# Feed-forward rows kept in DRAM by chunk of tokens instead of by feature group, with the order of all streams written anew

## The chip, the cores and the metric

The kernel runs on one core of a Trainium2 chip. The metric is device time in microseconds for one execution, as the median of several runs; lower is better. The core has a matrix engine (TensorE, shown as PE; its weight loads as PEld), a vector engine (VectorE, DVE), an activation engine (ScalarE, ACT), a general engine (GpSimd, POOL) and a queue processor (SyncE, SP). DMA transfers are issued here from SP, ACT and POOL and run on sixteen DMA engines.

## The reference

What is computed is the forward pass and the gradients of one block over 2048 tokens of 512 channels. The input is normalized; one branch is a long convolution whose kernel comes from a diagonal state space model of 128 states for each channel, the other a feed-forward network of 1792 features; the two are multiplied and added to the input. Cut to what matters:

```python
def _B_ref(x, w1, w2):
    h = jnp.einsum("bsd,df->bsf", x, w1)
    h = _silu(h)
    out = jnp.einsum("bsf,fd->bsd", h, w2)
    return out
...
x = A_u
xn = _layernorm(x, axis=-1)
s = _A_ref(xn, A_A_re, A_A_im, A_B_re, A_B_im, A_C_re, A_C_im, A_log_dt, A_Dskip)
g = _silu(_B_ref(xn, B_w1, B_w2))
return x + s * g
```

`_A_ref` builds the convolution's kernel K from the parameters, and convolves it with its input by Fourier transforms. The outputs are the block's result and the gradients with respect to the input, the seven parameter arrays of the state space model, the skip vector `Dskip`, and the two weights `w1` and `w2`, for a given `grad_out`.

## The kernel before

The 2048 tokens are worked on in eight chunks of 256, the 1792 features in 14 groups of 128, the 512 channels in four blocks of 128. The program is a set of some forty-five streams, each a Python generator that issues a small step of work at every call. `play` (L120) walks through a string of letters and advances the stream of each letter by one step. So the string `PLAN` is the order in which every engine's queue is filled. It has seven sections, one for each phase. Engines run in their own queue's order and wait for each other through semaphores. Two more tables go with it: `SLOTS` says which of a tag's buffers each new tile takes, and `WAYS` says for each copy out of PSUM that goes through `Evac` (L107) whether ACT (A, issued at L116) or DVE (D, issued at L117) makes it.

The pre-activations h of the feed-forward network are needed three times, and are kept in a DRAM tile `k.Hd` in between:

- Written in the forward pass. `gen_ffn_fwd` (stream F) computes, for each chunk c, h transposed: features on the partitions and 256 tokens along the row, in tiles `hT` of eight groups and then six (L768 the products, `Evac` the copies, L776 the SiLU). After each tile, L778 stores it to `k.Hd` from POOL's queue (`k.st` is POOL's `dma_start`). That is 16 stores.
- Read by chunk in the gradient of the activations. `gen_da_loads` (stream a) loads tiles `dhT` of the same shape from SP's queue at L1141: 16 loads, with three buffers for the tiles of eight groups and two for those of six. Stream s turns them into the slope of SiLU on ACT (L1151), stream A multiplies them on DVE with the products of L1173 (L1176) and stores the result to `k.DHd` from SP (L1180), and stream x takes them to the gradient of the input (L1197).
- Read by feature group in the gradient of `w2`. `gen_dw2_loads` (stream h) loads, for each of the 14 groups, all 2048 tokens as one tile `h_in` at L1216, from SP's queue, into three buffers. Stream t turns each with TensorE in two halves of eight blocks (L138) and applies SiLU on ACT (L1227); stream w multiplies them with the output's gradient (L1236) and stores `out_11`.

Before the change `k.Hd` has the shape [14 groups, 128 partitions, 2048 tokens]. A store or load by chunk touches, for each partition and each group, a run of 256 tokens in DRAM, which is 512 bytes; a load by group touches one run of 2048 tokens, 4096 bytes, for each partition.

Other streams that the prediction names: V copies the products of the state space gradient out of PSUM (L1025), T multiplies them on DVE (L1042, L1046), S sums them on TensorE (L1062), and Z makes the parameter gradients from the sums (DVE L1086 to L1113, ACT L1121, POOL stores at L1124). Stream Y loads and turns tables for V. Streams g and v make the gradient of `w1` (loads with transposition of `k.DHd` at L1251, products at L1265). Streams i, k and m are the backward pass of the normalization at the very end; k runs on DVE (L1306, L1307, L1309) and ACT (L1313). Streams R, C and B make the convolution's kernel rows, the forward convolution and its gradient, J the turned chunks of the input, W the turned weights and d the turned output gradients. The kernel rows (stream R, L651 to L659) are made eight channel groups at a time, before and after.

Each stream's steps are the same before and after the change; only the places of the steps in the string are not.

Of the kernel before, what the change touches and what calls it, by code (L numbers as in the profile page):

```python
# [18 lines left out]
P = 128  # L19
# [5 lines left out]


PLAN = """
222315555166p567155737777617777p63677J360710734777p07J6760F3p67677J64FF7687J7F667F86676261F873776F03778FFFF47FF66667FF76
347674678F73F586F47688758/XXJPFJFFFXXXFXFXPXFQPFPFXFFPFFPFFFFPPFFFFF9FQJUUXFQQXJPXXQRQQXQQQFRFQPRRFRXFXFRXXPRFFPRRFFFPQF
UQRXXFFQFXFQFQPQQFUQFQFQRFFXFQXPXFPFXQRPXFRXRPRRRRRXPQRPFFFRPFRRRRRXFRFRXCQXXXQFXQQXQRQFQQRFQXXFRRUXFPRRQCRPFCPPFCFCCFCC  # L30
PCFQFJFQCQCCFQQFCQPFQCRRCCQQRCCFPXCXFQPCPJFXRFCFXRCFCPFCXFXFFFRCFRFQFRCFRFFRXFCXPCRRQQXFXRFCQCFRQFQQQRCRCRRQCQRCRRRCFQPC
XCXRRFCRRJPPXPXXRQJFXRPXQCQFQXFXFXQPQCRRQFQPQCPCRXFCCRFFQFCCCFCPCCFFRFFUFFCQCFFFCRCRCFCQRCFCCCRJCCRCQCXPXFXPCQCXRPCRCQXC
FXFCRQQPCRQPJCFRQCRCRFXCQPQCCXFFRFRXRQRXRFFXQCXRCPFFCRRFCFCRRCRFFFXXCQQCFCCFQFQQXFRXRRFRCCQCFUFXCQCQRCCQCRRRCRJCCRQRRCRJ
CRCCCRUCFCRCCRCRRFCRRFCC/CFCFCGGCGFGCCCGFFFCCFGCCCGGCGFCCFFCFGFCCCCGCFGGFWCCGFGCCCGHFCFCGHFCCFCGGFHCFCCGGCFCGCGCGCCCFCWG
CHWHWHWHCWCCCWWCDDGWCHCLCWMCWWWWDDWWDWDDWDWWWWLMWCDWDDWDLGDMDLMLWWM/DDEDDDDaaasdooEdWDdoDdDABAADooAABADsBDADAAaDAABAlABB
BBDDAABABAsDDAAaoBAABBBADODABBABOEBBABABDBBoDDBxsBDBBxBoBxBAAdBBBOoBAsAlDBOABxBdOEDBDoOlBxBaDxOoOBxOxODDBBDxxDBlABBsxBoB
ABBxoBAADBOAAOaBaoDBBBBBoDDBaAABBDAoDAdDBBAADBAdBABBAEAABABsBBAAODOABoOABBDBABEADODoDOxoDBAlDsOBoADDOAxAdBDDBOAoAdBADABB
BoxBAoOADsDxBABOOBBADBDOlaBoAAxOBDBDooxBBxBBaBAOxDxBABDoBDOsODBDADxBEBOBAAOdBOBoBABxxOAoAaBdABAoBBExBOAsBBBDDOBAaOBAxBAB
BBxxBOBAaBsBAaABxABABABBBBABxBAAAAABBBddBxsBABBBABBBAxBABsBAABB/NNAYNYNYANxxNAAVVsaYVVAdVVAVVVAdYVTAAYYAAVVVVVxAATAATsxV
VAAAxATVNxAAATNNAxTTTNNVAVVVTSSxVTAYAVxTTxVYVYxYTYSTTVVYTxVASVT/TVVVhYSVVVhTVVtttVtTVVVTSTYwVTttthVVVVYTYSwTtwVtVTVTTTVS  # L40
VwTVVTwYTZVStVtgZSTVTVtwNZYNwNgYTVYNVTwTTTvhSvtYvYthVtTVVTYZvtTSVwYvVVVVVZTSvVVYVSVZNvvTVZVZtTtTgYVTgVVwtVVTVStTVwTVwVTZ
vTwSVVZTVNVYTTVTVTwvZNVZTZZvSYVhZNYvTtYYvZNTSVVtvhtTtTYShYwTVVYvVtSVvVYVTVTtYZwTVVZwhTTTVTVVtSVYTtVwVVVtTSTwVtVVSVVSVwVV
YvTYVtTwTTtttZgTVwZTVZTZTTYYtvZVVgSVSZTTVZVZwVYZgvSZZYYhvvTSVtTZVhgVvvTwVTZVTVVwTVTZSTtgTTZTSvZgZTvtvStSwhtZwvZttwZZZtvZ
tZZvZZvvZZgZtv/ivwtkhkvvwkwitkivwvtvkkwmvtkmkvvktwgvvwvvitmkhmkikvvmkkmvgmtiwktkvkkvmgkwkvtvtwmmkivmmkvkkwkvvitmkmkmkkvv
vmkmmwmkkwvmmvwvmvvvmvm
""".replace("\n", "").split("/")
# [15 lines left out]

WAYS = """J=DDAADDAD;
F=ADAAAAAAADDAAADAAADAAAAAAAAAAADAAAAAAAAAAAAAADDAAADAAADADADDAAAAAADDAAAA;
X=AAAAAAAAAAAAAAAAAAAAAAAAAAAAAAAA;
U=AD;
R=AAAAAAAAAAAAAAADAADAAAAADAAAAAAA;
C=ADDADAAAAAAAAAAAAAAADDAAAAAAAADDAAAAADADAAADDADAADADDDADAAAAAAAA;  # L70
W=DDDDDDDDDDDDDD;
D=AAAADDAAAAAAAAADAAAAAAAAAAAAAAAAAADAAAAA;
d=DDDAADAA;
B=AAAAAAAAAAADAADAAAAAAAAADADAAAAAAAAAAAAADAAADAAAAAAADAAA;
x=AADDDAADAAAA;
V=ADDDAAADDDAAAAAADDAAAAADDAAAAAAAAAAAAAAAAAAAAAAAAAAAAAAAAAAAAAAA;
Y=AAAAADAA;
w=AAAAAAAADDAAAA;
v=DDDAAADDAAAAADDAAAAAAAAAAAAA"""
# [674 lines left out]
def gen_ffn_fwd(k):  # L754
    nc, fp = k.nc, k.fp
    D, FT, DK, T = k.D, k.FT, k.DK, k.T
    for c in range(T // 2):
        cs = slice(256 * c, 256 * c + 256)
        XTv = k.XT.pop(c)[:].rearrange("p (t k) n -> p t k n", k=DK)
        aT = fp.tile([P, FT, 256], BF16, name="aT", tag="aT", bufs=1)  # L760
        for f in range(FT // 2):
            if f in (0, 4):
                hT = fp.tile([P, 8, 256], BF16, name="hT", tag="hT", bufs=2)
            ps = k.pf.tile([P, 2, 256], F32, name="ps_h", tag="pf")
            for j in range(2):
# [4 lines left out]
            yield  # L770
            i = 2 * (f % 4)
            k.ev(hT[:, i:i + 2, :], ps[:])
            yield
            if f in (3, 6):
                f0, n = (0, 8) if f == 3 else (8, 6)
                nc.scalar.activation(out=aT[:, f0:f0 + n], in_=hT[:, 0:n], func=ACT.Silu)  # L776
                yield
                k.st(k.Hd[f0:f0 + n, :, cs].rearrange("f p n -> p f n"), hT[:, 0:n])  # L778
                yield
        late = c >= NS  # L780
        ob = k.do[:, 2 * c:2 * c + 2, :] if late else fp.tile([P, 2, D], BF16, name="ob", tag="ob", bufs=2)
        for t in range(2):
            ps = k.pf.tile([P, D], F32, name="ps_o", tag="pf")
            for ft in range(FT):
                nc.tensor.matmul(out=ps[:], lhsT=aT[:, ft, t * P:t * P + P], rhs=k.W2[:, ft, :],  # L785
                                 start=(ft == 0), stop=(ft == FT - 1))
            yield
            k.ev(ob[:, t], ps[:])
            yield
        if not late:  # L790
            k.st(k.Od[:, 2 * c:2 * c + 2, :], ob[:])
            yield
# [419 lines left out]
def gen_dw2_loads(k, fw):  # L1212

    for ft in range(k.FT):
        h = fw.tile([P, k.T, P], BF16, name="h_in", tag="h_in", bufs=3)
        k.nc.sync.dma_start(h[:].rearrange("p t n -> p (t n)"), k.Hd[ft])  # L1216
# [118 lines left out]
def kernel(ctx, tc, A_u, A_A_re, A_A_im, A_B_re, A_B_im, A_C_re, A_C_im, A_log_dt, A_Dskip, B_x, B_w1, B_w2, grad_out,  # L1335
           out_0, out_1, out_2, out_3, out_4, out_5, out_6, out_7, out_8, out_9, out_10, out_11):
    nc = tc.nc
    k = KCtx()
# [142 lines left out]
```

## Time and profile before

| what | value |
|---|---|
| runs of the kernel before | 576.57, 572.45, 576.95 us; median 576.57 |
| the profiled execution's own time | 576.9 us |
| its span, first to last instruction | 575.1 us |
| mean granted TensorE clock | 0.981 |
| DVE busy | 523.5 us (91%) |
| ACT busy | 442.6 us (77%) |
| POOL busy | 79.0 us (14%) |
| all DMA packets | 156643, 144.49 MB |

The profiled execution is 0.3 us above the median of the runs, and 1.8 us of it lie outside the span. A busy share is a mean over phases that have different limits; the prediction therefore reads the span in stretches. Idle time is given with what ended it ("releaser"). Some rows carry a line number of a helper: L116 and L117 are the ACT and DVE copies of `Evac` for all streams, L138 is the turning helper.

### The profile page before, as it was taken

What the parts mean: (1) busy time and instruction counts of PE and PEld (TensorE: products, weight loads), DVE (VectorE), ACT (ScalarE), POOL (GpSimd) and SP (SyncE); (2) the same over time, 40 slices, a digit from 0 to 9 for tenths busy, and PEclk for the clock granted to TensorE, in tenths of its full rate; (3) what the DMA queues carried; (4) which work ended last, traced back from release to release, by engine and by line L of the source; (5) the groups of instructions that cost most, each with busy time, mean ns of one, the idle gap of its engine ahead of it and who ended that gap; (6) DMA issues with size and microseconds to landing.
All of it is one profiled execution on the core that took longest, in us unless ns stands there. A gap on an engine that the chain in (4) does not pass through costs nothing.

```text
span 575.1 us, 14488 instructions
## 1 busy us (share of the span) xinstructions
PE 528.4 (92%) x5982; PEld 396.0 (69%) x6008; DVE 523.5 (91%) x821; ACT 442.6 (77%) x541; POOL 79.0 (14%) x164
## 2 busy tenths in 40 slices
PE   0788998999999999999999999999999999899895
PEld 0545777587777675877687866776678687767573
DVE  8999998999899969999999899869999999894984
ACT  6989998999988569998888876773667677642473
POOL 5341101011101021000000000000000300333031
PEclk9889998999999999999999999999999999999798
DMA  9988797798997999898789799898999989999653
GB/s 240 310 309 227 226 256 261 264 258 266 331 239 247 334 276 364 253 283 286 232 241 315 220 293 294 216 221 229 251 226 260 241 205 222 222 210 264 169 177 111
DMA packets 156643, 144.49 MB, mean 251 GB/s; under 512 B 83488, under 2 KB 132896, under 8 KB 153504
## 3 DMA queue, kind: packets, MB, share of 16 engines
q1 hardware_dynamic: 146816, 120.74, 76.0%
q0 software_dynamic: 6640, 19.67, 10.0%
q10 hardware_dynamic: 3120, 3.15, 1.7%
q8 instruction: 47, 0.77, 0.5%
q14 instruction: 20, 0.16, 0.1%
HBM read 62.78 MB, written 59.25 MB: 212 GB/s over the span
## 4 chain that ended last, share of the span: by engine, by line
PE 57%; DVE 15%; ACT 7%; issue 7%; DMA 7%; SPq 4%; POOL 2%; ACTq 0%; DVEq 0%; POOLq 0%
PE ps_da L1173 8%; PE ps_dx L1197 7%; PE ps_w L1236 7%; PE ps_w L1265 6%; PE ps_o L785 3%; PE ps_h L768 3%; PE ps_i L451 3%; PE pt_t L138 3%; PE ps_s L406 3%; DMA sp_in<-Ud 3%; PE ps_i L464 3%; PE ps_v L1025 2%; PE psS L1062 2%; PE ps_k L657 2%; PE ps_s L434 2%
## 5 line engine op out<-in xcount | busy, mean ns | idle before, releaser
L116 ACT CAST dA<-ps_s 128x1024 bf16<-128x1024 f32 x90 | 89.1, 1029 | 9.6 <-PE ps_s L434 4.1
L768 PE MATMUL ps_h<-XT,W 128*128 128x256 bf16 x448 | 59.4, 284 | 6.0 <-DVE XT L117 4.9
L1265 PE MATMUL ps_w<-dh_tok,xn 128*128 128x256 bf16 x448 | 55.2, 280 | 3.2 <-ACT o L116 3.2
L1173 PE MATMUL ps_da<-doT,W 128*128 128x256 bf16 x448 | 56.1, 273 | 0.4 <-DVE dhT L1176 0.4
L768 PEld LDWEIGHTS <-W 128*128 128x128 bf16 x448 | 44.1, 102 | 14.5 <-issue 7.1
L785 PE MATMUL ps_o<-W,aT 128*128 128x512 bf16 x212 | 50.8, 387 | 1.7 <-issue 0.5
L116 ACT CAST Vb<-ps_v 128x672 bf16<-128x672 f32 x54 | 38.5, 732 | 17.6 <-PE ps_v L1025 13.7
L1265 PEld LDWEIGHTS <-xn 128*128 128x128 bf16 x448 | 44.1, 100 | 10.1 <-issue 3.6
L1197 PE MATMUL ps_dx<-W,dhT 128*128 128x512 bf16 x224 | 51.0, 379 | 0.0
L1236 PE MATMUL ps_w<-YD,a_tok 128*128 128x512 bf16 x210 | 49.1, 379 | 0.7
L116 ACT CAST dB<-ps_i 128x1024 bf16<-128x1024 f32 x41 | 40.7, 1027 | 9.1 <-PE ps_i L451 9.1
L1173 PEld LDWEIGHTS <-W 128*128 128x128 bf16 x448 | 41.3, 98 | 8.3 <-issue 2.6
L1176 DVE TENSOR_TENSOR dhT<-ps_da,dhT 128x512 bf16<-128x512 f32 x56 | 37.7, 685 | 6.2 <-PE ps_da L1173 5.7
L785 PEld LDWEIGHTS <-aT 128*128 128x128 bf16 x224 | 21.6, 100 | 26.7 <-issue 3.1
L1197 PEld LDWEIGHTS <-dhT 128*128 128x128 bf16 x224 | 21.2, 98 | 24.1 <-issue 1.2
L1236 PEld LDWEIGHTS <-a_tok 128*128 128x128 bf16 x224 | 21.6, 98 | 23.2
L1227 ACT ACTIVATE a_tok<-pt_t 128x1024 bf16<-128x1024 bf16 x28 | 28.7, 1036 | 7.3 <-PE pt_t L138 7.3
L406 PEld LDWEIGHTS <-TF 128*128 128x128 bf16 x384 | 24.9, 100 | 12.1 <-ACT TF L288 4.4
L477 DVE TENSOR_TENSOR cm<-sp_in,dA 128x2048 bf16<-128x2048 bf16 x24 | 29.3, 1220 | 2.6 <-DMA sp_in<-Ud 1.7
L116 ACT CAST o<-ps_w 128x256 bf16<-128x256 f32 (+1 forms) x33 | 14.9, 451 | 20.0 <-PE ps_w L1265 10.7
L479 DVE TENSOR_TENSOR sp_in<-sp_in,dA 128x2048 bf16<-128x2048 bf16 x24 | 29.3, 1223 | 0.6
L584 ACT ACTIVATE sn<-V 128x1920 bf16<-128x1920 int16 x16 | 29.0, 1816 | 1.1 <-DVE V L580 1.0
(241 smaller groups left out, 1234.1 us busy)
## 6 DMA issues: line engine op xcount, KB each, us to landing
Yd<-YD SPq DMA_DIRECT2D x8, 1024.0 KB, 5.7
sp_in<-Ud SPq DMA_DIRECT2D x8, 1024.0 KB, 7.8
h_in<-Hd SPq DMA_DIRECT2D x14, 512.0 KB, 5.1
Ed<-ds SPq DMA_DIRECT2D x8, 672.0 KB, 6.3
Eb<-Ed SPq DMA_DIRECT2D x8, 672.0 KB, 5.1
Hd<-hT POOLq DMA_DIRECT2D x8, 512.0 KB, 7.7
Ud<-dA SPq DMA_DIRECT2D x8, 512.0 KB, 8.5
KXd<-dA SPq DMA_DIRECT2D x4, 1024.0 KB, 4.7
```

The costliest lines, as they stand in the source:

```text
L116: return self.nc.scalar.copy(out=out, in_=in_)
L406: nc.tensor.matmul(out=ps[:, j], lhsT=k.TF[:, 8 * h + j, c, :], rhs=U(8 * h + j), start=True, stop=True)
L477: TT(out=t2[:], in0=b[:, :, gs], in1=a[:, 1:2, gs].to_broadcast([P, 2, n, P]), op=ALU.mult)
L479: TT(out=b[:, :, gs], in0=b[:, :, gs], in1=a[:, 0:1, gs].to_broadcast([P, 2, n, P]), op=ALU.mult)
L584: nc.scalar.activation(out=sn[:, 0:n], in_=low, func=ACT.Sin, scale=-2 * PI_LO / 2.0 ** PB)
L768: nc.tensor.matmul(out=ps[:, j], lhsT=k.W1[:, dk, ft * P:ft * P + P], rhs=XTv[:, :, dk, :], start=(dk == 0), stop=(dk == DK - 1))
L785: nc.tensor.matmul(out=ps[:], lhsT=aT[:, ft, t * P:t * P + P], rhs=k.W2[:, ft, :], start=(ft == 0), stop=(ft == FT - 1))
L1173: nc.tensor.matmul(out=ps[:, j], lhsT=k.W2[:, ft, dk * P:dk * P + P], rhs=dTv[:, :, dk, :], start=(dk == 0), stop=(dk == DK - 1))
L1176: nc.vector.tensor_tensor(out=dh[:, i0:i0 + 2, :], in0=ps[:], in1=dh[:, i0:i0 + 2, :], op=ALU.mult)
L1197: nc.tensor.matmul(out=ps[:], lhsT=dhs[ft // 8][:, ft % 8, t * P:t * P + P], rhs=k.W1[:, :, ft * P:ft * P + P], start=(ft == 0), stop=(ft ...
L1236: nc.tensor.matmul(out=ps[:], lhsT=at[:, t, :], rhs=k.do[:, t, :], start=(t == 0), stop=(t == k.T - 1))
L1265: nc.tensor.matmul(out=ps[:], lhsT=k.xn[:, t, dk * P:dk * P + P], rhs=dh[:, t].rearrange("p j n -> p (j n)"), start=(t == 0), stop=(t == k ...
```

## The change

`k.Hd` gets the shape [8 chunks, 128 partitions, 14 groups, 256 tokens]. The store of a tile `hT` and the load of a tile `dhT` are then one run for each partition in DRAM: 4096 bytes for eight groups, 3072 for six. The load of one feature group, `h_in`, becomes eight runs of 512 bytes for each partition, one from each chunk. The bytes are the same everywhere, as are the queues: POOL for the stores, SP for both loads. No other instruction is added or taken away.

```diff
@@ gen_ffn_fwd @@
-                k.st(k.Hd[f0:f0 + n, :, cs].rearrange("f p n -> p f n"), hT[:, 0:n])
+                k.st(k.Hd[c][:, f0:f0 + n, :], hT[:, 0:n])
@@ gen_da_loads @@
-            k.nc.sync.dma_start(dh[:, 0:n], k.Hd[f0:f0 + n, :, 256 * c:256 * c + 256].rearrange("f p n -> p f n"))
+            k.nc.sync.dma_start(dh[:, 0:n], k.Hd[c][:, f0:f0 + n, :])
@@ gen_dw2_loads @@
-        k.nc.sync.dma_start(h[:].rearrange("p t n -> p (t n)"), k.Hd[ft])
+        k.nc.sync.dma_start(h[:].rearrange("p (c u) n -> p c (u n)", u=2), k.Hd[:, :, ft, :].rearrange("c p n -> p c n"))
@@ kernel @@
-    k.Hd = dr.tile([k.FT, P, L], BF16, name="Hd")
+    k.Hd = dr.tile([8, P, k.FT, 256], BF16, name="Hd")
```

With it the whole of `PLAN`, `SLOTS` and `WAYS` is written anew. The letters of each stream are the same in number over all sections, but some steps cross a boundary: section 4 (the fifth) holds 35 steps of V and 18 of T instead of 30 and 17, and section 5 has 101 of V instead of 106. The start of section 5, where the loads `h_in` begin, as an example:

```diff
-TVVVhYSVVVhTVVtttVtTVVVTSTYwVTttthVVVVYTYSwTtwVtVTVTTTVS
+hTVVTYVVSThYVtTtttSVYTTtVVSTYhwtVSTTTwVVVTtYVSwVVtTVVwhV
```

In `WAYS`, D stands 94 times before and 105 times after, of 454 copies. By stream, the copies that DVE makes: J 5 to 6, F 15 to 18, R 3 to 5, C 17 to 16, d 4 to 3, B 7 to 11, V 10 to 12, Y 1 to 2, w 2 to 4, v 7 to 5; the others keep their numbers.

More of the change, by code (lines that the diff above doesn't have):

```diff
@@ L32 @@
[L32 to L41, printed above, removed]
@@ new lines @@
+F75FF738F7FFFJ76F7F6778FJ34/XFXFFFXXXXXXPPPFPF9PFFPFFFPQFFFFXPFFXQQFUQFQQFFFQQUFPFFXRQXQXXPFXFFQXXRFQRPXFPRRXRUFFFFRPXFU
+QRXQRFFRXQFPFRFFQXFFJFQFQXQQFXXPFQQFFXPQRPRRPRXRRJFRRRFPFXQPRFPRRRRRRFFFXFXQRFFQCPXQXXXQQQRXFQFQRQFPRFRRXFCXCPPCRFURCCQC
+QQCCFCQFCFFQPCQQCPFCCQPRRQRCPJCCCQQJXFXFRCPCXFQFFCCCXFXFRXFFCFCFXFXRFRRFRCFRXFQFRFQRCQQCFQQRPCQRFFRCQRXFCRPCCQRQRCFRRCRX
+RPPCXRQRPCXFRXJRUPCJCRXQFXFXXPXQFCQXCPQQFXFQFPFRRCRQFCCQCFFCQQCCCPQFFFFRFFCRCFFCFCRRFCRCRJCCPCCCRCPCXFXFPXRCQXRCFXXQCRQC
+PQCQQPPQJCFXFCPRCQRCCRFQRCRCCFRXRFCRFXRQFQFXFXRCFXCCPRFCFRRCFFURFXRQXCCQQFCFQCCFXFRRJXQCRRFQCCFXQFQRQCCCCCCRRCRRRQCRRCCR
@@ L58 @@
+010110101101011010;dft.t4=010010101010;gate.g=10237456;gate.S=01;da.dhT8=01201201;da.dhT6=01010101;da.doT=10101010;go.go
+_s=01010101;go.go_r=010101;dftb.w8b=1010;go.go_g=01010101;go.go_x=01201201;da.pd_s=101010101010;sb.YT=2012012012012012;s
 b.Eb=01010101;sb.Gb=01010101;sb.Vb=0101010101010101;sb.Tp=0101010101010101;sb.Sa=1010;fw.h_in=01201201201201;fw.a_tok=10
-101010101010;fw.o11=01201201201201;fw.dh_tok=0120120;sb.g_acc=0101;fw.o10=0101010;lw.pd_l=012301;lw.Gt=01230123;lw.m=010
+101010101010;fw.o11=01201201021021;sb.g_acc=0101;fw.dh_tok=0120120;fw.o10=0101010;lw.pd_l=012301;lw.Gt=01230123;lw.m=010
@@ L60 @@
 101;lw.o1=12031203
 """.replace("\n", "").split(";") if x)
[L65 to L66 removed]
+WAYS = """J=DDADDDAD;
+F=DAAAAAAAADDDADAAAAAAAAAAAAAAAAAADAAAAAAAAAAAADDAAAADAADDADADAAAADDDDDAAA;
 X=AAAAAAAAAAAAAAAAAAAAAAAAAAAAAAAA;
 U=AD;
[L69 to L70 removed]
+R=AAAAAAAAAAAAAADDAAAAAAAADAADAADA;
+C=ADDADAAAAAAAAAAAAAAADDAAAAAAAADDAAAAADADAAADADAAADADDDADAAAAAAAA;
@@ L71 @@
 W=DDDDDDDDDDDDDD;
 D=AAAADDAAAAAAAAADAAAAAAAAAAAAAAAAAADAAAAA;
[L73 to L79, printed above, removed]
+d=DDAADAAA;
+B=AAAAAAAAAAADDADAAADAAAAADAAAAAADAAAADADAAAAADAAAAAAAADAD;
+x=AAADDAAADADA;
+V=ADADDDDAAAAAAAADAAAADAADAAAAAADAAADAAAAAAAAAAAAAAAAAADAAAAADAAAA;
+Y=AADDAAAA;
+w=DDAADAAAADAAAA;
+v=ADADAAAAAAAADDAAAAAAAAAAAADA"""
```

35 lines of the change are left out of this document (19 added, 16 removed).

## The prediction

> **What bounds the kernel now.** I read the page's busy times first, then the busy time of each engine in stretches, because a share of the whole span hides which engine is full where.
>
> ```profile
> span 575.1 us, 14488 instructions
> PE 528.4 (92%) x5982; PEld 396.0 (69%) x6008; DVE 523.5 (91%) x821; ACT 442.6 (77%) x541; POOL 79.0 (14%) x164
> ```
>
> PE and DVE are busy for nearly the same time. The table by stretches has a column for the length, then the busy time of PE, PEld, DVE, ACT and POOL with instruction counts, the granted clock, the DMA share and GB/s.
>
> ```profile
> 0.00:43.00 43.00, 22.94 (x154) 15.40 (x156) 40.07 (x103) 35.98 (x54) 18.96 (x68) 0.92 0.92 286
> 43.00:225.00 182.00, 171.12 (x2130) 129.24 (x2139) 170.26 (x217) 163.85 (x182) 22.23 (x28) 0.99 0.88 271
> 225.00:300.00 75.00, 73.75 (x977) 55.74 (x975) 73.36 (x100) 68.90 (x72) 2.18 (x4) 1.00 0.82 261
> 300.00:365.00 65.00, 65.00 (x778) 46.47 (x777) 60.36 (x81) 49.60 (x54) 4.30 (x8) 1.00 0.90 283
> 365.00:410.00 45.00, 43.76 (x451) 32.07 (x450) 37.70 (x53) 24.69 (x26) 0.00 (x0) 1.00 0.92 211
> 410.00:490.00 80.00, 78.67 (x856) 61.69 (x863) 79.07 (x122) 59.56 (x91) 9.02 (x17) 1.00 1.04 238
> 490.00:530.00 40.00, 37.81 (x383) 29.33 (x386) 28.25 (x63) 17.46 (x30) 14.30 (x26) 1.00 0.99 234
> 530.00:575.20 45.20, 35.36 (x265) 26.06 (x265) 34.42 (x88) 22.56 (x37) 7.96 (x14) 0.88 0.54 154
> ```
>
> The start belongs to DVE (40.07 of 43). From 43 to 225 PE, DVE and ACT are all at nine tenths or more. From 225 to 490 PE is idle for only 75.00+65.00+45.00+80.00 less 73.75+65.00+43.76+78.67, which is 3.8 us, and DVE is as full as PE in 225 to 300 (1.6 us idle) and 410 to 490 (0.9 us). Between, in 300 to 410, DVE has 4.6+7.3 = 11.9 us to spare. So no transfer of `Hd` has much to give: where `dhT` is used, PE hardly ever waits. The list of waits for 225 to 400 says the same; its longest one of DVE is for PE, and no row of it, nor of that for 400 to 535, names `dhT<-Hd` or `h_in<-Hd` (columns: total us, times, longest).
>
> ```profile
> DVE dhT L1176 <- PE ps_da L1173: 5.7, 9, 2.3
> ```
>
> At the end there is one visible stall, read in the timeline (start, duration, instruction, idle time before it):
>
> ```profile
> 519.57 0.87 ACT L1121 ACTIVATE gout<-pt_g 128x384 bf16<-128x384 bf16 x2
> ...
> 529.42 0.69 DVE L1306 SCALAR_TENSOR_TENSOR pd_l<-pd_l,ds 128x512 bf16<-128x512 bf16 x1 [4.52 <-DMA out_dram<-gout]
> ...
> 532.44 1.52 ACT L1313 ACTIVATE pd_l<-pd_l,m,rstd 128x512 bf16<-128x512 bf16 x2 [6.44 <-DVE m L1309]
> ...
> 534.48 3.57 PE L1265 MATMUL ps_w<-dh_tok,xn 128*128 128x256 bf16 x16 [3.24 <-ACT o L116]
> ```
>
> Stream k's first DVE step waits until the last parameter gradients have left (529.42), ACT's step of k at L1313 waits for that, ACT's copies of PSUM queue up behind it, and PE stands 3.24 us for a free PSUM buffer.
>
> **The layout.** The issues that touch `Hd` (columns: count, KB each, median us from issue to landing):
>
> ```profile
> h_in<-Hd SPq DMA_DIRECT2D x14, 512.0 KB, 5.1
> Hd<-hT POOLq DMA_DIRECT2D x8, 512.0 KB, 7.7
> dhT<-Hd SPq DMA_DIRECT2D x8, 512.0 KB, 6.8
> dhT<-Hd SPq DMA_DIRECT2D x8, 384.0 KB, 5.5
> ```
>
> Here is a clean pair: `h_in` and the large `dhT` move the same 512 KB on the same queue, one in 4096-byte runs, one in 512-byte runs. The difference, 6.8-5.1 = 1.7 us, is my price of short runs for 512 KB, bounded from below by zero (some of it may be the company that each kept) and from above by the same 1.7. The change exchanges the two: 16 loads `dhT` become 1.7 or, by size, 1.3 us quicker, 8x1.7+8x1.3 = 24.0 us of landing time, and 14 loads `h_in` become 1.7 us slower, 14x1.7 = 23.8 us. The layout therefore does not make short runs vanish; it carries them from the stretch 225 to 410 to that from 410 on, and also takes them out of the stores.
>
> The stores: POOL's issue costs 891 ns for the scattered form, 541 ns for contiguous rows.
>
> ```profile
> L778 POOL DMA_DIRECT2D Hd<-hT x16 | 14.3, 891 | 65.7 <-ACT hT L116 42.4 <-DVE W L651 6.8 <-ACT ds L116 5.8
> L1330 POOL DMA_DIRECT2D out_dram<-o x8 | 4.3, 541 | 10.5 <-DVE o L1328 7.5 <-DVE m L1309 2.5 <-DVE mx L1309 0.4
> ```
>
> That is 16x0.35 = 5.6 us less on POOL. I cost it at nothing: the 16 issues follow 65.7 us of POOL's own idle time, and nobody waits for `Hd` there. The faster `dhT` I cost at nothing too: the work that hides it is PE's, idle 1.25 us in 225 to 300 and not at all in 300 to 365. [...]
>
> The slower `h_in` can matter, because some loads were only just in time. The first, third and fourth issue on SP, and the first turn of each on PE:
>
> ```profile
> 407.51 0.32 SPq L1216 DMA_DIRECT2D h_in<-Hd  x1
> 414.59 0.58 SPq L1216 DMA_DIRECT2D h_in<-Hd  x1
> 430.15 1.66 SPq L1216 DMA_DIRECT2D h_in<-Hd  x2
> ...
> 413.10 1.06 PE L138 MATMUL pt_t<-ident,h_in 128*128 128x128 bf16 x16
> 421.42 0.61 PE L138 MATMUL pt_t<-ident,h_in 128*128 128x128 bf16 x8
> 436.45 0.61 PE L138 MATMUL pt_t<-ident,h_in 128*128 128x128 bf16 x8
> ```
>
> The leads are 5.6, 6.8 and 6.3 us. With 6.8 us to land, the first would be 1.2 us late, the fourth 0.5. The new string puts 13 letters instead of 10 between the first load and its turn, and 28 and 47 instead of 14 and 3 for the third and fourth, so only the first stays tight: I take +1.0 us, between 0 and 1.7. [...]
>
> **The copies that change engine.** DVE makes 11 more copies. Its prices (min/median/max in ns):
>
> ```profile
> L117 DVE CAST hT<-ps_h x15: 673/682/692, 20.4 to 217.1; 128x512 bf16<-128x512 f32 x15
> L117 DVE CAST Vb<-ps_v x10: 847/850/858, 380.0 to 426.1; 128x672 bf16<-128x672 f32 x10
> L117 DVE CAST o<-ps_w x9: 418/421/682, 437.3 to 524.2; 128x256 bf16<-128x256 f32 x7, 128x512 bf16<-128x512 f32 x2
> L117 DVE CAST dB<-ps_i x7: 1223/1224/1225, 205.7 to 369.5; 128x1024 bf16<-128x1024 f32 x7
> L117 DVE COPY XT<-pt_t x5: 675/683/683, 13.7 to 196.5; 128x1024 bf16<-128x1024 bf16 x5
> L117 DVE CAST KE<-ps_f x1: 552/552/552, 128.7 to 128.7; 128x384 bf16<-128x384 f32 x1
> L117 DVE COPY YT<-pt_y x1: 692/692/692, 468.2 to 468.2; 128x1024 bf16<-128x1024 bf16 x1
> ```
>
> In sections 0 to 2: F 3x0.68, J 0.68, R two small copies at no more than the 0.55 of the wider KE, less one of C at 1.22: +2.6 us. In section 3: B three wide ones at 1.22 and one of 0.68, less one of d at 0.68: +3.7. In section 5: V 2x0.85, w 3x0.68, Y 0.69, less two of v at 0.42: +3.6. Section 6 has one of w less, -0.7. Together +9.2 us on DVE, and about 8 us less on ACT, which limits nothing alone. What of it reaches the end depends on DVE's spare time: 43 to 225 has 182.00-170.26 = 11.7 us for the 2.6, 300 to 410 has 11.9 for the 3.7. I cost both at nothing; if DVE's gaps there cannot be used because they stand behind PE (the 5.7 us for L1176), up to 6.3 us come back. The 3.6 us fall on the stretch 410 to 490, which has 0.9 to spare: +2.7.
>
> **The end.** From the last transposes of Z to ACT's first L1313, and on to the first block of products that lacks a PSUM buffer, both strings give PE four blocks of v and one of w; the old one adds two turns of eight, the new one four. Such a turn is 0.61 us in the rows above, so PE has 1.2 us more to do: I take 1.2 off the stall of 3.24, which can also go altogether or stay.
>
> The sum, on the profiled execution's 576.9 us: +1.0+2.7-1.2 = +2.5, or 579.4. The three runs have the median 576.57, 0.3 lower, so I say **579 us**, for a kernel whose engines have 4% to 8% of room and whose order changes everywhere. About 1% is what a measurement of this kernel can tell from no change: the three runs alone reach from 572.45 to 576.95. One per cent of 576.6 is 5.8 us, so the bounds are 570.8 and 582.3.
>
> **Rivals.**
> *DVE becomes the bound (slower).* All of the 9.2 us reaches the end, because in-order queues cannot use the spare time where it lies: 576.9+9.2+1.0-1.2 = 585.9, or 586. For it: DVE is at 98% in 225 to 300 and 99% in 410 to 490. Against it: 11.9 us of idle time between. It decides from the point where more than 5.6 us of the 9.2 are not absorbed. Chance 0.22.
> *Late `h_in` (slower).* The DMA share is already about 1.0 from 410 to 530. For 400 to 535 and 225 to 400 the SP queue's packets, MB and share of sixteen engines are:
>
> ```profile
> q1 hardware_dynamic: 52630, 28.19, 92.8%
> q1 hardware_dynamic: 51973, 39.74, 77.9%
> ```
>
> 14x(1024-128) = 12,544 packets are added to the first and 16 loads' worth taken from the second. If four loads come 1.7 us late each, 6.8 us, the time is 577+6.8, or 584. Against it: the longer leads of the new string. Chance 0.12.
> *Faster.* PE stood idle for 10.9 us in 43 to 225, 2.2 in 490 to 530 and 3.24 in the last stall; a string made for quicker stores and loads may close half of these 16.3 us: 576.9-8.2 = 569. For it: lighter POOL and 24 us of landing time less before 410. Against it: none of those gaps is put down to `Hd`. [...] Chance 0.18.
> *Nothing arrives.* All transfers stay hidden and the new order is as good as the old: 577. Chance 0.13.
>
> **The numbers.** The forecast itself has 0.35 (own range 575 to 582). Within 1%: 0.35+0.13 = 0.48; slower 0.22+0.12 = 0.34; faster 0.18. The range 569 to 587 reaches from the faster rival to the first slower one and leaves out some 0.2 at both ends.
>
> **What would show it.** Right: `dhT<-Hd` lands near 5 us and `h_in<-Hd` near 7; L778 at about 540 ns; DVE busy near 532 us; PE's idle time from 225 to 365 unchanged. Wrong: a wait on `h_in` before L138 of more than 2 us in all; DVE idle in 300 to 410 as large as before with a longer span (then the first rival); PE's idle time in 43 to 225 below 6 us (then the faster one), or above 17, for which I have no mechanism.

## The result, and the profile after

| | median | runs | lowest to highest |
|---|---|---|---|
| before | 575.63 us | 13 | 571.40 to 578.14 |
| after | 579.09 us | 13 | 577.11 to 581.63 |

The ratio of all runs is 1.0069, with a 95% interval of 1.0045 to 1.0092: slower by 0.7% or 4.0 us (the two medians differ by 3.5), inside the bound of 1%. The forecast of 579 us came true almost to the digit, and that is luck: it was +2.4 us on a median of before that is 0.9 lower in the 13 runs, and most steps behind it failed, as the traces show. Errors of both signs cancel. The profiled execution of after took 581.63 us with a span of 579.8; that of before 576.9 and 575.1. So the traces differ by 4.7 us, 1.2 more than the medians.

First the page of after, its span and busy times:

```profile
span 579.8 us, 14494 instructions
PE 528.4 (91%) x5982; PEld 395.3 (68%) x6008; DVE 530.5 (91%) x832; ACT 437.6 (75%) x530; POOL 71.7 (12%) x164
```

DVE has 7.0 us more (523.5 before), ACT 5.0 less, POOL 7.3 less. PE does the same work in the same time. Next the stretches of after (length, then busy time of PE, PEld, DVE, ACT, POOL, the clock, DMA share, GB/s):

```profile
0.00:43.00 43.00, 23.58 (x142) 15.56 (x144) 40.39 (x105) 35.54 (x53) 18.04 (x68) 0.84 0.95 283
43.00:225.00 182.00, 170.84 (x2141) 129.47 (x2150) 171.07 (x219) 162.83 (x178) 15.83 (x28) 0.99 0.92 274
225.00:300.00 75.00, 73.51 (x976) 55.96 (x975) 72.91 (x101) 68.93 (x72) 2.16 (x4) 1.00 0.79 262
300.00:365.00 65.00, 65.00 (x778) 46.23 (x776) 62.10 (x82) 51.62 (x54) 4.32 (x8) 1.00 0.84 274
365.00:410.00 45.00, 42.43 (x425) 30.29 (x423) 35.77 (x50) 20.40 (x23) 0.00 (x0) 1.00 0.92 209
410.00:490.00 80.00, 73.64 (x829) 59.10 (x836) 77.52 (x122) 52.58 (x80) 7.23 (x13) 1.00 0.98 219
490.00:530.00 40.00, 39.42 (x383) 29.19 (x385) 35.18 (x71) 21.04 (x36) 14.66 (x27) 1.00 0.98 225
530.00:575.20 45.20, 39.99 (x324) 29.49 (x325) 35.52 (x89) 24.68 (x40) 9.50 (x17) 1.00 0.68 200
```

Compare 410 to 490 with the row of before. PE's idle time there rises from 1.33 to 6.36 us, while DVE is *less* busy (77.52 against 79.07) and the DMA share is lower. So neither DVE nor the DMA engines are fuller than before in this stretch, and PE waits all the same. PE's own timeline names the waits. Before, from 403 to 430 (start, duration, instruction, and in brackets the idle time before it and what ended it):

```profile
410.27 0.45 PE L1025 MATMUL ps_v<-Gb,YT 128*128 128x168 bf16 x4 [0.56 <-ACT Vb L116]
411.06 0.45 PE L1025 MATMUL ps_v<-Gb,YT 128*128 128x168 bf16 x4 [0.34 <-ACT Vb L116]
414.74 0.45 PE L1025 MATMUL ps_v<-Gb,YT 128*128 128x168 bf16 x4 [0.30 <-DVE Vb L117]
```

And after:

```profile
410.83 0.68 PE L1025 MATMUL ps_v<-Gb,YT 128*128 128x168 bf16 x7 [1.03 <-ACT YT L116]
412.07 0.45 PE L1025 MATMUL ps_v<-Gb,YT 128*128 128x168 bf16 x4 [0.56 <-ACT Vb L116]
412.69 0.45 PE L1025 MATMUL ps_v<-Gb,YT 128*128 128x168 bf16 x4 [0.17 <-ACT Vb L116]
415.65 0.74 PE L1025 MATMUL ps_v<-Gb,YT 128*128 128x168 bf16 x8 [1.33 <-DVE Gb L1015]
416.95 0.45 PE L1025 MATMUL ps_v<-Gb,YT 128*128 128x168 bf16 x4 [0.56 <-ACT Vb L116]
426.92 0.74 PE L1025 MATMUL ps_v<-Gb,YT 128*128 128x168 bf16 x8 [1.01 <-DVE Vb L117]
```

All these waits belong to stream V: for a table to be turned (YT), for the scaled gradient (Gb), or for a PSUM buffer to be copied out (Vb). No row names `h_in` or `Hd`. The issues of after that touch `Hd` (KB each, median us to landing), from the view of its DMA queues:

```profile
h_in<-Hd SPq DMA_DIRECT2D x14, 512.0 KB, 6.0
Hd<-hT POOLq DMA_DIRECT2D x8, 512.0 KB, 5.8
dhT<-Hd SPq DMA_DIRECT2D x8, 512.0 KB, 5.9
...
Hd<-hT POOLq DMA_DIRECT2D x8, 384.0 KB, 6.3
dhT<-Hd SPq DMA_DIRECT2D x8, 384.0 KB, 4.9
```

The loads by group take 6.0 instead of 5.1 us, the large loads by chunk 5.9 instead of 6.8 and the small ones 4.9 instead of 5.5. The large stores take 5.8 instead of 7.7, the small ones 6.3 instead of 5.5. These medians hold the layout and the new order together; the experiments take them apart. The issue of a store comes from the row of L778 of after (min/median/max ns):

```profile
L778 POOL DMA_DIRECT2D Hd<-hT x16: 538/547/739, 37.8 to 222.4; - x16
```

The largest surprise is the end. The program's last line makes each engine's queue drain. Before, the drains of POOL and SP (min/median/max ns; the span of starts):

```profile
L1476 POOLq DRAIN  x3: 40/93/6604, 567.7 to 574.9; - x3
L1476 SPq DRAIN  x3: 7/7/7, 571.2 to 574.6; - x3
```

After:

```profile
L1476 POOLq DRAIN  x3: 40/93/8401, 570.7 to 579.6; - x3
L1476 SPq DRAIN  x3: 7/7/7, 573.8 to 579.3; - x3
```

The longest of the three DRAINs of POOL starts together with POOL's last store and holds the program's end: SP reaches its own at 571.2 before and 573.8 after, but the spans end at 575.1 and 579.8. The DRAIN took 6.60 us before and 8.40 us after. The last stores themselves, in POOL's timeline, first before, then after:

```profile
567.77 0.54 POOL L1330 DMA_DIRECT2D out_dram<-o  x1 [0.28 <-DVE o L1328]
```

```profile
570.70 0.54 POOL L1330 DMA_DIRECT2D out_dram<-o  x1 [1.05 <-DVE o L1328]
```

So the 4.7 us between the two spans split without a rest: 2.93 because the last store is issued later, 1.80 because the DRAIN behind it is longer.

### The profile page after: what moved, and what is told of

It is laid out like the page before. It is cut to its first block, busy times and chain, and to the rows that moved or that the text cites. A ratio compares the mean times of both kernels' runs of the same rounds, so it can differ in the third digit from the quotient of the medians.

```text
span 579.8 us, 14494 instructions
## 1 busy us (share of the span) xinstructions
PE 528.4 (91%) x5982; PEld 395.3 (68%) x6008; DVE 530.5 (91%) x832; ACT 437.6 (75%) x530; POOL 71.7 (12%) x164
## 5 line engine op out<-in xcount | busy, mean ns | idle before, releaser
L116 ACT CAST Vb<-ps_v 128x672 bf16<-128x672 f32 x52 | 36.8, 728 | 30.3 <-issue 13.8
L1173 PE MATMUL ps_da<-doT,W 128*128 128x256 bf16 x448 | 56.8, 273 | 0.0
L1265 PE MATMUL ps_w<-dh_tok,xn 128*128 128x256 bf16 x448 | 52.5, 272 | 1.0 <-ACT o L116 1.0
L1197 PE MATMUL ps_dx<-W,dhT 128*128 128x512 bf16 x224 | 51.0, 379 | 1.3 <-DVE dhT L1176 1.3
L1265 PEld LDWEIGHTS <-xn 128*128 128x128 bf16 x448 | 43.3, 98 | 7.1 <-issue 1.3
L1173 PEld LDWEIGHTS <-W 128*128 128x128 bf16 x448 | 41.4, 98 | 8.1 <-issue 1.6
L116 ACT CAST dB<-ps_i 128x1024 bf16<-128x1024 f32 x38 | 38.1, 1027 | 7.5 <-PE ps_i L451 7.1
L1197 PEld LDWEIGHTS <-dhT 128*128 128x128 bf16 x224 | 21.1, 98 | 25.6 <-DVE dhT L1176 1.6
L1025 PE MATMUL ps_v<-Gb,YT 128*128 128x168 bf16 x256 | 27.0, 236 | 6.1 <-ACT Vb L116 1.6
L1151 ACT ACTIVATE dhT<-dhT 128x2048 bf16<-128x2048 bf16 (+1 forms) x16 | 27.4, 1712 | 3.1 <-DMA dhT<-Hd 2.1
```

Source lines behind the costliest of these rows:

```text
L116: return self.nc.scalar.copy(out=out, in_=in_)
L1151: k.nc.scalar.activation(out=dh[:], in_=dh[:], func=ACT.Derivative_silu)
L1173: nc.tensor.matmul(out=ps[:, j], lhsT=k.W2[:, ft, dk * P:dk * P + P], rhs=dTv[:, :, dk, :], start=(dk == 0), stop=(dk == DK - 1))
L1197: nc.tensor.matmul(out=ps[:], lhsT=dhs[ft // 8][:, ft % 8, t * P:t * P + P], rhs=k.W1[:, :, ft * P:ft * P + P], start=(ft == 0), stop=(ft ...
L1265: nc.tensor.matmul(out=ps[:], lhsT=k.xn[:, t, dk * P:dk * P + P], rhs=dh[:, t].rearrange("p j n -> p (j n)"), start=(t == 0), stop=(t == k ...
```

## The experiments

Twelve kernels ran, each against the kernel before on the same chip. The sections of `PLAN` are numbered from 0, as in the change's description. Diffs are against the kernel after unless they say otherwise.

**Layout alone, order alone.** The first pair separates the two halves of the change. Layout alone is the kernel before with only the four changed lines on `Hd`:

```diff
-    k.Hd = dr.tile([k.FT, P, L], BF16, name="Hd")
+    k.Hd = dr.tile([8, P, k.FT, 256], BF16, name="Hd")
...
```

> The order, the buffers and the copies of the kernel before, with the new shape of Hd alone. If the layout carries the loss (theory L), this run is 3 us or more slower than before, ratio 1.005 or above, with h_in landing near 6.0 us and the first turn of h_in after 413.1 us. If the loss is in the order (theory P, the pile-up of V's steps at 405 to 430 us) or in the copies moved to DVE (theory D), the ratio is 0.998 to 1.002; the early leads of h_in, 5.6 us against about 6.0 to land, cost at most 0.5 us. If quicker dhT and stores give something, the ratio is below 0.998.

Order alone is the kernel after with those four lines put back:

```diff
-    k.Hd = dr.tile([8, P, k.FT, 256], BF16, name="Hd")
+    k.Hd = dr.tile([k.FT, P, L], BF16, name="Hd")
...
```

> The new order, buffers and copies, with the old shape of Hd. Theories P and D: as slow as the changed kernel, ratio 1.005 to 1.009, and PE idle 5 us or more in 405 to 430 us. Theory L: back to 0.998 to 1.002.

Measured: layout alone 1.0068 (1.0039 to 1.0096), order alone 1.0093 (1.0058 to 1.0129). Each half alone costs what both together cost; they don't add up, and no theory had foreseen both results. In layout alone `h_in` lands in 6.3 us instead of 5.1, and the large `dhT`, now in contiguous runs, in 7.0 instead of 6.8. In layout alone the late load that I had feared does occur (PE's timeline of this run):

```profile
438.73 0.62 PE L138 MATMUL pt_t<-ident,h_in 128*128 128x128 bf16 x8 [1.33 <-DMA h_in<-Hd]
```

The new order, with longer leads, has no such wait, with either layout.

**The copies on DVE.** If the 11 copies given to DVE cost time, giving them back should gain. First all of `WAYS` as before, then only the streams V, Y, w and v:

```diff
-V=ADADDDDAAAAAAAADAAAADAADAAAAAADAAADAAAAAAAAAAAAAAAAAADAAAAADAAAA;
-Y=AADDAAAA;
-w=DDAADAAAADAAAA;
-v=ADADAAAAAAAADDAAAAAAAAAAAADA"""
+V=ADDDAAADDDAAAAAADDAAAAADDAAAAAAAAAAAAAAAAAAAAAAAAAAAAAAAAAAAAAAA;
+Y=AAAAADAA;
+w=AAAAAAAADDAAAA;
+v=DDDAAADDAAAAADDAAAAAAAAAAAAAA"""
```

> The changed kernel with the WAYS of the kernel before for all streams: 94 instead of 105 copies on DVE, at the same places in the order. Theory D (copies on DVE: 9 us of work moved, of which 2.7 reach the end): 2 to 4 us faster than the changed kernel, ratio to before 0.999 to 1.003. Theory P: no gain, ratio 1.005 to 1.009. Above that, if the choice of engine fits its own order only.

> The changed kernel with the old WAYS of the streams V, w, Y and v alone, which takes four copies off DVE after 410 us, about 3.6 us of its work. Theory D, in the form of the prediction: 2.7 us faster than the changed kernel, ratio 1.001 to 1.004, and DVE less than 77 us busy in 410 to 490 us. Theory P: within 1 us of the changed kernel, ratio 1.005 to 1.009, with the waits of ps_v in 405 to 430 us unchanged in kind.

Measured: 1.0367 (1.0324 to 1.0410) and 1.0152 (1.0112 to 1.0192). Both are slower than the kernel after, and the second lies above both ranges that were expected. In it DVE is busy for only 73.64 of the 80 us from 410 to 490, and PE for 74.95 at a clock of 0.98: less work on DVE, hardly a gain on PE. So the number of copies on DVE is not what costs time in this order; `WAYS` fits the order that it was written for. The edit also moves the D's to other copies of a stream, and no run took single copies off DVE at their places.

**The closing drain.** If the DRAIN of POOL holds the end, then stores that leave on another queue let it begin earlier. Three of the eight stores of L1330 and the last one of L1241 go to SP, in the kernel after and in the kernel before:

```diff
-        k.st(k.outs[11][ft * P:ft * P + P, :], ob[:])
+        (nc.sync.dma_start if ft == k.FT - 1 else k.st)(k.outs[11][ft * P:ft * P + P, :], ob[:])
...
-        k.st(k.o1_v[:, 2 * c:2 * c + 2, :], o1[:])
+        (nc.sync.dma_start if c >= 5 else k.st)(k.o1_v[:, 2 * c:2 * c + 2, :], o1[:])
```

> The changed kernel, where the last four stores of POOL's queue (the normalization's chunks 5 to 7 and the last block of the gradient of w2) are issued from SP instead. Theory E (the end is POOL's last issue plus its closing DRAIN, 8.40 us with the new layout and 6.60 with the old, plus 0.7 us): the last issue of POOL moves from 570.7 to about 563 us, the DRAIN is over before SP has seen the last stores land at about 574, and the span becomes 575 instead of 579.8 us, 4 to 5 us less; ratio to before 0.998 to 1.002. If the end is set by PE's last products and their stores, less than 1 us is gained, ratio 1.005 to 1.008.

> The same edit in the kernel before. Theory E: POOL's last issue at about 560 us, the DRAIN over by 567, the end at the landing of SP's last store at 571 us and 0.7 behind it: 2.5 to 3.5 us faster than before, ratio 0.994 to 0.996, since its DRAIN was 1.8 us shorter. Otherwise less than 1 us, ratio 0.998 to 1.000.

Measured: 573.04 us, 0.9958 (0.9928 to 0.9987), from the kernel after; and 569.54 us, 0.9917 (0.9885 to 0.9949), from the kernel before, the fastest of all. The drains of the first:

```profile
L1476 POOLq DRAIN  x3: 40/102/8074, 560.9 to 571.5; - x3
L1476 SPq DRAIN  x3: 7/7/7, 570.9 to 571.3; - x3
```

The long DRAIN now begins at 560.9, ends after 8.07 us near 569, and no longer matters; SP's at 570.9 decides, and the span ends at 571.8. The drains of the second:

```profile
L1476 POOLq DRAIN  x3: 40/93/6274, 558.1 to 570.3; - x3
L1476 SPq DRAIN  x3: 7/7/7, 569.8 to 570.1; - x3
```

Both gained more than was expected. The first is 8.0 us shorter in the traces, where 4 to 5 were expected; 5.3 of them are the DRAIN's lead over SP in the trace of after (570.7+8.4 = 579.1 against 573.8). SP itself is 2.9 us earlier, and 2.7 us of that were gained before the last L1173, in an execution with a mean granted clock of 0.994 instead of 0.981. By medians the second gains 5.3 us, by traces 4.5. The DRAIN's lead over SP explains 3.1 of them (567.7+6.6 = 574.3 against 571.2 in the trace of before); PE's last products also came 2.2 us earlier, which the edit doesn't explain.

The lengths sort all fourteen traces of this study without exception. With POOL's stores as they were, the DRAIN took 6.60 us in both traces with the old layout and 8.40 in all seven with the new one, whatever the order. With four stores fewer it took 6.27 in two and 8.07 in three. The 1.80 us follow the layout, the 0.33 the four stores that left POOL. Why a drain at the end should remember how `Hd` was stored 350 us earlier no trace shows.

**Which sections.** Two hybrids of the orders, both with the new layout: new sections 0 to 3 with old 4 to 6, and the reverse. `SLOTS` and `WAYS` go with the section that uses them, and one step each of streams d and s is moved so that every stream stays complete. The first hybrid, at the start of section 4:

```diff
-NNAYNNYYNxNxAxxVaVVAVAVAYAYVVAVYVVsTAYdTAAxA
+NNAYNYNYANxxNAAVVsaYVVAdVVAVVVAdYVTAAYYAAVVVVV
...
```

> The new layout, with the new order, buffers and copies in sections 0 to 3 and the old ones in sections 4 to 6. Theory P (the order's loss is PE's idle time at 365 to 430 us, where the new sections 4 and 5 begin): only the layout's 1.8 us of DRAIN are left and perhaps the 1 us that the layout alone cost elsewhere, ratio 1.002 to 1.006, and PE idle 1.5 to 2.5 us in 410 to 490 us. If the loss comes from the early sections: 1.007 or above.

The second, at the start of section 0:

```diff
-1222315355466p657717p77777572666371J6J77040776
+222315555166p567155737777617777p63677J36071073
...
```

> The new layout, with the old order, buffers and copies in sections 0 to 3 and the new ones in sections 4 to 6. Theory P: PE idle 5 us or more in 410 to 490 us, as slow as the changed kernel, ratio 1.006 to 1.010. If the loss comes from the early sections: 1.002 to 1.006.

Measured: 1.0006 (0.9975 to 1.0037) for new early sections, 1.0132 (1.0094 to 1.0170) for new late ones. The stretches of the first:

```profile
365.00:410.00 45.00, 42.48 (x435) 31.64 (x434) 38.55 (x54) 21.81 (x26) 0.00 (x0) 1.00 0.95 214
410.00:490.00 80.00, 79.07 (x862) 61.28 (x860) 77.95 (x123) 57.64 (x87) 10.62 (x20) 1.00 1.07 232
```

PE is idle for 0.93 us from 410 to 490, at a DVE load above that of after. The second has 74.99 of 80 there, like after. The first is faster than either theory had it, the second slower. With layout alone and the kernel after, the two complete a square, all four with the new layout: the new sections 0 to 3 gain 0.6% with old late sections (1.0068 to 1.0006) and with new ones (1.0132 to 1.0069), and the new sections 4 to 6 lose 0.6% with old early sections (1.0068 to 1.0132) and with new ones (1.0006 to 1.0069). Each of these differences is uncertain by some 0.4%. So with this layout the two parts of the new order cancel: the order's loss lies in the late sections, and the early ones give as much. With the old layout the whole new order costs 0.9% (order alone); its parts were not run there.

**Section 4 by itself.** Against the first hybrid, section 4 is new too, and the steps that it does early, five of V and one of T, are taken out of the old section 5 (one step of S is put in):

```diff
-NNAYNYNYANxxNAAVVsaYVVAdVVAVVVAdYVTAAYYAAVVVVV
+NNAYNNYYNxNxAxxVaVVAVAVAYAYVVAVYVVsTAYdTAAxAVA
...
-TVVVhYSVVVhTVVtttVtTVVVTSTYwVTttthVVVVYTYSwTtw
+ShYSVhTVVtttVtTVVVTSTYwVTttthVVVVYTYSwTtwVtVTV
...
```

> The new layout, the new order in sections 0 to 4 and the old one in 5 and 6, with the five steps of V and one of T that the new section 4 has more taken off the start of section 5, and one of S added there. Beside the run with sections 0 to 3 alone (1.0006). Theory P in the form that V's early steps in section 4 pile up: 3 us or more slower than that, ratio 1.005 or above, with PE idle 2.5 us in 365 to 410 and 3 us or more in 410 to 490. If the loss lies in the new section 5 (its first turns of h_in come late): ratio 0.999 to 1.003.

Measured: 581.99 us, 1.0124 (1.0077 to 1.0171). One new section more than the first hybrid, and the time goes from 575.52 to 581.99 us. Its stretches:

```profile
365.00:410.00 45.00, 40.87 (x402) 29.73 (x400) 35.64 (x52) 21.65 (x25) 0.00 (x0) 1.00 0.98 209
410.00:490.00 80.00, 78.28 (x852) 63.11 (x859) 76.54 (x119) 54.37 (x83) 8.12 (x15) 0.96 1.00 223
```

PE is idle for 4.13 us in 365 to 410, more than expected, but for only 1.72 in 410 to 490, where 3 or more were expected; there its clock was granted at 0.96. To see where the time goes, here is when the last matmul of L1173 starts in these traces, and the time from there to the last of L1197, from that to the last of L1025, and from that to the last of L1265. The next two columns are PE's idle time between the last L1173 and the last L1025, and between that and the last L1265. The last one is an estimate of what PE lost in both stretches at a granted clock of 0.50: half of the time that it worked there. (The three kernels at the foot follow below.)

| kernel | order of sections 0-3, 4, 5-6 | last L1173 | to L1197 | to L1025 | to L1265 | idle to L1025 | idle to L1265 | clock |
|---|---|---|---|---|---|---|---|---|
| before | old, old, old | 400.4 | 6.7 | 96.4 | 65.0 | 3.3 | 3.9 | 2.9 |
| layout alone | old, old, old | 401.0 | 6.6 | 97.1 | 64.8 | 3.3 | 3.3 | 2.9 |
| before, close on SP | old, old, old | 399.9 | 6.6 | 96.1 | 63.7 | 2.6 | 3.6 | 1.5 |
| new early | new, old, old | 398.0 | 6.6 | 96.8 | 63.1 | 3.1 | 2.8 | 1.7 |
| section 4 | new, new, old | 396.4 | 9.2 | 100.5 | 65.9 | 5.2 | 5.5 | 5.0 |
| new late | old, new, new | 399.8 | 9.1 | 100.4 | 61.7 | 5.8 | 0.8 | 1.6 |
| order alone | new, new, new | 400.4 | 9.2 | 100.2 | 61.9 | 7.2 | 1.1 | 0 |
| after | new, new, new | 399.8 | 9.1 | 100.0 | 62.1 | 7.4 | 1.5 | 0 |
| after, close on SP | new, new, new | 397.1 | 9.1 | 100.0 | 61.7 | 7.0 | 0.8 | 0 |
| layout alone, close on SP | old, old, old | 402.0 | 6.6 | 98.9 | 62.1 | 5.0 | 3.7 | 0 |
| new early, close on SP | new, old, old | 398.0 | 6.7 | 98.7 | 65.4 | 5.0 | 4.3 | 2.8 |
| order alone, close on SP | new, new, new | 398.5 | 8.8 | 100.5 | 62.1 | 5.8 | 1.6 | 1.7 |

The column to L1197 goes with section 4: 6.6 or 6.7 us with the old one, 8.8 to 9.2 with the new one, whatever stands before and behind it (and 10.9 in the two runs with old `WAYS` in the new order). The next one is 96.1 to 97.1 with the old section 4 (98.7 and 98.9 in the two runs with late loads, below) and 100.0 to 100.5 with the new one. These lengths are not all loss, since work moves across the marks: of the 2.4 us more to L1197, PE is idle for 0.6; the rest is products of V that now run there. The idle time says more. Up to the last L1025 it is 2.6 to 3.3 us with old sections 4 to 6 (5.0 with late loads), 5.2 with section 4 new, and 5.8 to 7.4 with all late sections new. So of the 4.1 us between before and after, the new section 4 brings about half, as far as single traces can tell, and the rest comes with the new section 5. The run with section 4 alone loses more by what follows: 3.3 us more by the clock than the first hybrid, 2.9 of it behind its gaps near 410 (last section), and 2.7 us more idle time on the way to the last L1265, where the stall is 4.80 us instead of 2.44. These and the 2.1 us of idle time are 8.1 us, against 7.5 between the two spans.

The new section 4 mixes V with the last products of L1197 and holds five more steps of V; while their copies and multiplications are under way, PE has little else queued. That it is these five steps and not another difference of section 4 was not tried by itself. The column to the last L1265 is 61.7 to 62.1 with new sections 5 and 6, and 62.1 to 65.9 with old ones.

**Do the good parts add up?** Three last runs put the close on SP into the other combinations: old order with the new layout; new early sections with the new layout; new order with the old layout. The edit is that of the fourth diff above.

> The old order with the new layout, and the last four stores of POOL issued from SP, so that the DRAIN is over before SP's last store lands. If the DRAIN's 1.8 us are the layout's whole cost in the old order, this run equals the old kernel with the same edit (0.9917): ratio 0.989 to 0.994. If the rest of the 3.9 us that the layout alone cost is real (late h_in, more packets behind 410 us), ratio 0.995 or above.

> The new order in sections 0 to 3, the old one in 4 to 6, the new layout, and the last four stores from SP. The run without the last edit had 1.0006, its DRAIN ended 4.8 us behind SP's. Theory E: 4.5 to 5.5 us less, ratio 0.990 to 0.993, about as fast as the old kernel with the same edit. If the early sections of the new order are really better by what the 1.8 us of DRAIN hid, it is below that: 0.987 to 0.990.

> The new order with the old layout, and the last four stores from SP. The fourth corner with DRAIN out of the way. If the layout has no other effect than on the DRAIN, it equals the changed kernel with the same edit (0.9958): ratio 0.993 to 0.999. If the new order needs the new layout (quicker stores and dhT loads), it is 1.000 or above.

Measured, with the two runs of the close from above and the four kernels without it:

| order | layout | POOL's stores as they were | four stores on SP |
|---|---|---|---|
| old | old | 1 | 0.9917 (0.9885 to 0.9949) |
| old | new | 1.0068 (1.0039 to 1.0096) | 1.0025 (0.9995 to 1.0054) |
| new early | new | 1.0006 (0.9975 to 1.0037) | 0.9993 (0.9966 to 1.0021) |
| new | old | 1.0093 (1.0058 to 1.0129) | 1.0009 (0.9968 to 1.0049) |
| new | new | 1.0069 (1.0045 to 1.0092) | 0.9958 (0.9928 to 0.9987) |

The close gains between 0.1% and 1.1% in the five pairs. Once the drain is out of the way, each full order is best with its own layout, clearly so for the old one; for the new one the intervals overlap. For the old order the waits say a part of why. Those of the run with the new layout, from 400 to 535 (total us, times, longest):

```profile
PEld L138 <- DMA h_in<-Hd: 1.9, 2, 1.1
PE pt_t L138 <- DMA h_in<-Hd: 1.4, 2, 0.9
PEld L990 <- DMA Yn<-Yd: 0.4, 1, 0.4
PEld L1025 <- DMA YT<-Yd: 0.4, 1, 0.4
```

With the old layout and the same close there is no row on a load at all. PE's waits come to 1.4 us for `h_in` and some tenths for Yn and YT, whose loads share SP's queue. These are about half of the 3.3 us between the two spans (573.9 and 570.6). By medians the two kernels differ by 6.5 us, so most of what the new layout costs the old order here is not explained. The new early sections, which should have come to 0.990 to 0.993 with the close, gained next to nothing from it: in the traces PE's last L1265 started at 568.8, against 564.5 without the close. Some of that is again waits on `h_in` (0.87 and 0.45 us), some a stall of 3.68 instead of 2.44 us before L1265 near 534, with a clock at half rate behind it (last section). Why that execution was later before the edit's place is even reached was not settled; the effects of single edits here carry an uncertainty of some 3 us when they are added up.

## Why the prediction was right in the sum

**The ledger.** My sum was +1.0 for the first load, +2.7 for DVE, -1.2 for the tail. By the ratios above it is: the layout +0.7% in the old order, the new early sections -0.6%, the new late ones +0.6%, some 4 us each. That is one way to add up; with the order first it is +0.9% for the order and -0.2% for the layout, so the two are not independent. In the traces of before and after, PE's idle time between the last L1173 and the last L1025 rises by 4.1 us; from there to the last L1265 it falls by 2.4, and the 2.9 us lost to the clock fall away. The early gain doesn't show in this pair, since the execution of after had the lower clock in the first 43 us (0.84 against 0.92). POOL's last store is issued 2.9 us later, and the DRAIN adds 1.80: 4.7, the difference of the spans.

**The layout's prices.** POOL's issue at 547 ns (forecast 540) came out as said, and nobody gained from it. The loads by chunk did not come out: my pair promised 5.1 and 4.2 us for the two sizes, and they took 5.9 and 4.9; in layout alone the large ones took 7.0, no less than before, and only in the new order did 7.2 (order alone) become 5.9. So the pair was not clean: in the old order its 1.7 us were the company that the large loads keep, not their short runs. For `h_in` I took all of the 1.7 us, which was too high. With the layout alone its median rose by 1.2 us in the old order (5.1 to 6.3) and by 0.5 in the new one (5.5 in order alone, 6.0 after).

**The first load, +1.0.** It failed as a term of this change. The first issue on SP and the first turn on PE, after:

```profile
409.31 0.38 SPq L1216 DMA_DIRECT2D h_in<-Hd  x1
```

```profile
417.24 1.06 PE L138 MATMUL pt_t<-ident,h_in 128*128 128x128 bf16 x16
```

The load landed 4.0 us after its issue (4.1 before), not the 6.8 that I charged it, so it would have been in time with the old lead of 5.6 too. The lead is now 7.9 us, above the longest landing of 7.1, because the waits of V push the turn back. The mechanism is real, as layout alone shows with 1.33 us, but at a later load, and the new order removes it. I had looked only at the letters between a load and its turn and took their length in time as unchanged.

**The copies, +2.7.** DVE's total was 530.5 us for the 532 forecast. That 9.2, or rather 7.0, us of copies press the stretch from 410 to 490 was the step that failed. PE did lose 5.0 us there, but with DVE less busy than before (77.52 against 79.07), and giving the copies back made it worse. What the runs show in its place is the order of the late sections, with PE idle for 4.1 us more up to the last L1025. Part of that comes with section 4; among its differences are the 35 steps of V instead of 30, which stand in the change's description and which I did not cost. That a loss of about this size was forecast is luck. The rival in which DVE becomes the bound falls too, though its sign appeared: DVE is idle for 12.1 us in 300 to 410 (11.9 before) and the span is longer. The sign was badly chosen, for DVE's spare time can stay unused without the copies being the cause; 586 us did not come, and fewer copies made the kernel slower.

**The tail, -1.2.** The direction was right and the size of the stall's change too small. The stall before L1265 went from 3.24 to 1.00 us (PE's timeline of after):

```profile
539.26 3.65 PE L1265 MATMUL ps_w<-dh_tok,xn 128*128 128x256 bf16 x32 [1.00 <-ACT o L116]
```

PE's idle time on the way to the last L1265 fell by 2.4 us (3.9 to 1.5). What I left out is the clock: behind this stall it cost 2.9 us before and nothing after. It was halved near 534 in six of seven traces with old sections 5 and 6, with stalls of 2.4 to 4.8 us, and in none of seven with new ones. The column to the last L1265 fell by only 2.9 us in all, because the new order leaves some 2 us more of PE's work to this stretch.

**POOL at nothing.** I costed POOL's stores at nothing because 65.7 us of idle time lay before them. That holds in the middle of the program. At its end POOL's DRAIN is the last event, and it grew by 1.80 us. The chain of waits, which ends with the last instruction that does work, doesn't show it; the rows of the closing line do.

**The rivals.** Late `h_in` came true for the old order only, at a fifth of its price. The faster rival was half there in size: the new early sections gain 0.6%, and in the table the last L1173 starts at 396.4 to 400.4 with them (median of seven 398.0) and at 399.8 to 402.0 with old ones (median of five 400.4). Its sign was not there: PE is idle for 11.2 us in 43 to 225, as before, where below 6 was asked. That quicker transfers make the gain is not shown: PE's idle time in 225 to 365 is 1.5 us, and was 1.2. The late sections and the drain take the gain back.

## What to carry to other kernels

Look at what ends the program, not only at what works last: if a queue's closing drain stands behind the last engine's work, move the last stores to another queue; here that was worth 0.8% on the kernel before and 1.1% on the kernel after, though next to nothing on one of the hybrids. When an order is written anew, count at every border of sections how many steps of each stream cross it, and try the sections one by one: here one half of the new order gave 0.6% and the other lost it, and the new section 4 without the sections written to follow it cost 1.2%. A layout, an order and a choice of engines fit each other, and one of them is judged only with the others that belong to it.

## What the hardware showed besides

**The clock falls to one half at a short stall, and not always.** From 534 to 542 before (length, PE busy, granted clock, DMA share, GB/s):

```profile
534.00:538.00 4.00, 3.52 (x18) 0.50 0.09 33
538.00:542.00 4.00, 3.95 (x28) 0.73 1.04 201
```

The stall of 3.24 us ends at 534.48; the clock is at 0.50 from about 533.4 for 6.8 us (stretches of 2 us from 532 on give 0.84, 0.50, 0.50, 0.50, 0.95, and 1.00 on both sides). From 534.48 on PE works in it, for 5.7 us; the first 16 products of L1265 take 3.57 us, where 16 at 529.33, at a clock of 1.00, took 1.91. Half of the 5.7 us, 2.9, is the estimate of what PE loses. After, with a stall of 1.00 us, it stays at 1.00. The gaps of V around 410 do the same in five of the eight traces with the new section 4. The run with section 4 alone, then after:

```profile
404.00:408.00 4.00, 2.97 (x26) 1.00 0.74 148
408.00:412.00 4.00, 3.18 (x32) 0.73 1.04 352
412.00:416.00 4.00, 3.00 (x27) 0.50 1.16 214
```

```profile
408.00:412.00 4.00, 2.48 (x22) 1.00 0.79 185
412.00:416.00 4.00, 2.42 (x34) 1.00 1.08 347
```

After has the larger gaps and keeps its clock; the other lost half of it for 6.8 us (from 409.9 by stretches of 1 us). By stretches of 2 us every halving at these two places comes to 3.4 or 6.8 us. It is 3.4 us in before with the close on SP and in new early, both near 534, and behind the gaps of V in new late, in order alone with the close on SP and in the two runs with old `WAYS`. It is 6.8 us near 534 in before, layout alone and new early with the close on SP, and at both places in the run with section 4 alone. Nor was PE idle throughout before the clock fell: in the 3.4 us before the loss near 410 in new late, section 4 and order alone with the close on SP, no single wait of PE was longer than 1.4 us, and PE worked for 1.5 to 1.7 us. What decides whether the clock falls is not shown. So a gap of PE at these two places costs its own length or, by the estimate above, up to 2.9 us more.

**POOL's closing DRAIN costs 6.3 to 8.4 us**, 0.33 us less when four stores leave its queue, and 1.80 us more with the 16 stores `Hd<-hT` in contiguous runs than in runs of 512 bytes, although those stores are quicker to issue (in the median 547 against 895 ns). The cause is open.
